# Two probability blocks of each group transposed by way of DRAM, and bucket codes put in place in three transfers a pair: attention and routed experts on one Trainium2 core

## The chip, the cores and the metric

One core of a Trainium2 chip runs the whole program. The metric is device time in microseconds of one launch, the median of several runs. The engines are TensorE (PE, with its weight loads PEld), VectorE (DVE), ScalarE (ACT), GpSimd (POOL) and SyncE (SP), which here only issues transfers.

## The reference

Attention over 4 batches of 8 heads, 768 rows of 64 numbers, restricted to keys in the same hash bucket, then a layer of 8 experts of which each token uses one. Core lines:

```
q_bits = (np.einsum('bhsd,dk->bhsk', q, proj) > 0)      # 6 bits a row; k the same
mask = q_bucket[:, :, :, None] == k_bucket[:, :, None, :]
scores = np.where(mask, scale * q @ k.T, -1e9)
attn = exp(scores - max) / (sum + 1e-9);  out = attn @ v
x = out as rows of 512
e = argmax(x @ w_gate);  y = gate * relu(x @ w1[e]) @ w2[e]
```

## The kernel before

The first 60% of the time is attention. It runs over 16 pairs of heads (4 batches of 4 pairs), each pair in two groups (g=0, 1) of 384 query rows. A group is six steps, one for each block of 128 queries of one head (`blocks`, L508). In pairs 1 to 14 the order of blocks (query block, head) is (1,0), (0,0), (1,1), (0,1), (2,0), (2,1), so the steps n=1 and n=3 hold query block 0 of both heads.

For a block, `scores` (L215) makes 128 x 768 scores on TensorE with four matmuls (L220, L221). L221 adds the low halves of the numbers and, in rows 64 to 75 of its operands q2 and k2, the bucket codes of queries and keys, times a large number, which is the mask. VectorE takes the row maximum (L223) and two small steps (L224, L225), ScalarE the exponential (L235). Scores have two PSUM buffers, so scores of block i+2 wait for the exponential of block i. The products with v (`av`, L272) need the probabilities with keys on partitions. There are two ways to turn them. `transposes` (L255): six 128 x 128 transposes on TensorE (L260), copied out of PSUM by ScalarE in two pieces (L263). `move` (L239): the exponential writes a tile `pd`, SyncE sends it to DRAM in four transfers (L245), fetches it back in another order in one (L248), and VectorE finishes with 32 x 32 transposes (L251, `turn`). Which steps of a group go the second way stands in `MOVES` (L503): step n=1 in pairs 1 to 14, with 28 blocks in all.

The main loop (L742 on) writes out the order on TensorE, VectorE, ScalarE and SyncE by hand. At step i it first calls the `turn` of a block moved five steps earlier, then the transfers that are due: out at the block's own step, back two steps later. Then come scores of block i+2, the exponential of i+1, the transposes of i, and in odd steps the products of one query block of the group before. At n=3 the finished output of an earlier group is transposed (L310) or, for a batch's last pair, its routing logits are made (L332), with small VectorE and ScalarE pieces of the routing in the steps that follow. At n=3 of early groups a transfer fills part of the expert rows with zeros (`prefill`, L116).

The operands of the next pair are prepared meanwhile (`PREPARE`). `pair_codes` at (g=0, n=1) computes codes on TensorE (L143), compares on VectorE (L145) and scales on GpSimd (L146). `q_operands` and `k_operands` split numbers on GpSimd. `code_rows` sends 12 rows of codes into each of q2 and k2 for each half of 384 columns, eight transfers a pair (L171).

Of the kernel before, what the change touches and what calls it, by code (L numbers as in the profile page):

```python
# [8 lines left out]
F32 = mybir.dt.float32  # L9
F32R = mybir.dt.float32r  # L10
# [8 lines left out]
P = 128  # L19
B, H, S, D = 4, 8, 768, 64  # L20
# [5 lines left out]
BITS = 6  # L26
NCODE = 2 * BITS
BIG = float(2.0 ** 60)
# [25 lines left out]
def bf(ap):  # L54
    return ap.bitcast(F32)
# [3 lines left out]
def lsh_attention_moe_kernel(ctx, tc, qkd, q2d, k2d, v, pjbd, wg, w1, w2, ident_in, tri_in, cols_in, eoff_in, ids_in, out):  # L59
    nc = tc.nc  # L60
    V, A, G, PE, SY = nc.vector, nc.scalar, nc.gpsimd, nc.tensor, nc.sync
# [6 lines left out]
    const = ctx.enter_context(tc.tile_pool(name="const", bufs=1))  # L68
    dram = ctx.enter_context(tc.tile_pool(name="dram", bufs=1, space=DRAM))
    xs = dram.tile([E * XROWS, ROW], F32, name="xs")  # L70
    moved = [dram.tile([P, 4, KQ], F32, name=f"moved{x}") for x in range(2)]
    writes = iter(range(6 * B * NPAIR))

    ident = const.tile([P, P], F32, name="ident")
    pj = const.tile([P, 32], F32, name="pj")
    cols = const.tile([P, 3], F32, name="cols")
# [16 lines left out]
    opp = att.enter_context(tc.tile_pool(name="opp", bufs=4))  # L93
# [23 lines left out]

    operands = {}
    codes = {}
    later = []  # L120

    def in_turn(ins):
# [15 lines left out]
    def pair_codes(pr):  # L138
# [6 lines left out]
        V.tensor_scalar(out=cr, in0=cps[:, 0:384], scalar1=0.0, scalar2=cols[:, 0:1], op0=ALU.is_gt, op1=ALU.subtract)  # L145
        in_turn(G.tensor_scalar(out=cr, in0=bf(cr), scalar1=cols[:, 1:2], scalar2=None, op0=ALU.mult))  # L146

    def q_operands(pr, hh):
        qk = operands[pr][0][hh][0]
        q1 = opp.tile([P, S], F32R, name="q1")  # L150
        q2 = opp.tile([P, S], F32R, name="q2")
        in_turn(G.tensor_copy(out=q1[0:D], in_=qk[0:D]))
        in_turn(G.tensor_tensor(out=q1[D:P], in0=qk[0:D], in1=bf(q1[0:D]), op=ALU.subtract))
        in_turn(G.tensor_copy(out=q2[0:D], in_=qk[0:D]))
        operands[pr][0][hh] += [q1, q2]

    def k_operands(pr, hh):
        qk = operands[pr][0][hh][0]
        k1 = opp.tile([P, S], F32R, name="k1")
        k2 = opp.tile([P, S], F32R, name="k2")  # L160
        in_turn(G.tensor_copy(out=k1[D:P], in_=qk[D:P]))
        in_turn(G.tensor_tensor(out=k2[0:D], in0=qk[D:P], in1=bf(k1[D:P]), op=ALU.subtract))
        in_turn(G.tensor_copy(out=k1[0:D], in_=qk[D:P]))
        operands[pr][0][hh] += [k1, k2]

    def code_rows(pr, hh):
        _, q2, _, k2 = operands[pr][0][hh][1:]
        for x in range(2):
            for j, t in enumerate((q2, k2)):
                r0 = 64 * x + 32 * hh + NCODE * j  # L170
                SY.dma_start(out=bf(t[D:KM, 384 * x:384 * x + 384]), in_=bf(codes[pr][r0:r0 + NCODE]))  # L171

    KM = D + NCODE

# [325 lines left out]
        return [logits, gather_heads, total]  # L500

    NPR = B * NPAIR
    MOVES = {}  # L503
    for pr in range(1, NPR - 1):
        for g in range(2):
            MOVES[(pr, g)] = (1,)

    def blocks(pr, g):  # L508
        if (pr, g) in MOVES:
            return [(1, 0), (0, 0), (1, 1), (0, 1), (2, 0), (2, 1)], ((1, 0, 2), (1, 2, 0))[len(MOVES[(pr, g)]) - 1]  # L510
        b = [(jj, hh) for jj in range(3) for hh in range(2)]
        return sorted(b, key=lambda x: x[::-1]) if (pr, g) == (0, 0) else b, (0, 1, 2)

# [18 lines left out]
    V.tensor_copy(out=run, in_=eoff[:, 1])  # L532
    SY.dma_start(out=ids, in_=ids_in)
    for hh in range(2):
        operands[0][0][hh] += [opp.tile([P, S], F32R, name=n) for n in ("q1", "q2", "k1", "k2")]
    PREPARE = (
        {(0, 1): [(pair_codes, ())], (0, 3): [(q_operands, (0,)), (k_operands, (0,))], (0, 5): [(q_operands, (1,)), (k_operands, (1,)), (code_rows, (0,))],
         (1, 1): [(code_rows, (1,))]},
        {(0, 0): [(q_operands, (0,))], (0, 1): [(pair_codes, ())], (0, 2): [(k_operands, (0,))], (0, 4): [(q_operands, (1,))],
         (0, 5): [(code_rows, (0,))], (1, 0): [(k_operands, (1,))], (1, 1): [(code_rows, (1,))]},  # L540
        {(0, 0): [(q_operands, (0,))], (0, 1): [(pair_codes, ())], (0, 2): [(k_operands, (0,))], (0, 3): [(q_operands, (1,))],
         (0, 5): [(k_operands, (1,)), (code_rows, (0,)), (code_rows, (1,))]})
    grp = {}
    soft = {}
    probs = {}
# [196 lines left out]
    for i, (pr, g, jj, hh) in enumerate(steps):  # L742
        n = i % 6
# [62 lines left out]
        if last:  # L806
            if n == 1:
# [4 lines left out]
                c0, c1, c2 = last_route(sums, o)  # L812
            elif n == 2:
                av(pr, g, 0, o)
                r = route(B - 1, 0)
# [203 lines left out]
    bufs = iter(range(1, 2 * E))  # L1019
# [119 lines left out]
    with tc.If(nc.values_load(spare[0:1, E:E + 1], min_val=0, max_val=max(most), skip_runtime_bounds_check_because=why) > 0):  # L1139
# [10 lines left out]
        for e in range(E):  # L1150
            rows_apart("xs", G.indirect_dma_start(out=xs, out_offset=bass.IndirectOffsetOnAxis(ap=row[:, e:e + 1], axis=0),
                                                  in_=pad.rearrange("p g w -> p (g w)"), in_offset=None))
# [7 lines left out]
def layout(q, k, v, proj, moe_w_gate, moe_w1, moe_w2):  # L1160
    import numpy as np
    a = {}
    qd = q.reshape(B * H, S, D).transpose(0, 2, 1)
    kd = k.reshape(B * H, S, D).transpose(0, 2, 1)
    a["qkd"] = np.concatenate([qd, kd], axis=1)
    a["q2d"] = np.concatenate([qd[0:2], qd[0:2]], axis=1)
    a["k2d"] = np.concatenate([kd[0:2], kd[0:2]], axis=1)
    a["v"] = np.ascontiguousarray(v.reshape(B * NPAIR, 2, NB, P, D).transpose(0, 3, 2, 1, 4).reshape(B * NPAIR, P, NB, 2 * D))
    pj = np.zeros((P, 32), proj.dtype)
    for hh in range(2):  # L1170
        for r in range(2):
            pj[hh * D:hh * D + D, hh * NCODE + r * BITS:hh * NCODE + r * BITS + BITS] = proj
    a["pjbd"] = pj
    wg = np.zeros((P, NPAIR, 32), moe_w_gate.dtype)
    for pi in range(NPAIR):
        for hh in range(2):
            wg[hh * D:hh * D + D, pi, hh * E:hh * E + E] = moe_w_gate[(2 * pi + hh) * D:(2 * pi + hh) * D + D]
    a["wg"] = wg

    a["w1"] = np.ascontiguousarray(moe_w1.reshape(E, NG, NDC, SQ, F).transpose(0, 2, 1, 3, 4).reshape(E, DM, F))  # L1180
    a["w2"] = np.ascontiguousarray(moe_w2.reshape(E, F, NG, NDC, SQ).transpose(0, 1, 3, 2, 4).reshape(E, F, DM))
    a["ident"] = np.eye(P, dtype=np.float32)
    a["tri"] = np.triu(np.ones((P, P), np.float32), 1)
    cols = np.zeros((P, 3), np.float32)
    cols[:, 1] = 1.0
    for g in range(4):
        cols[32 * g + BITS:32 * g + NCODE + BITS, 0] = 1.0
        cols[32 * g + NCODE:32 * g + 2 * NCODE, 1] = BIG
    cols[D:D + BITS, 2] = cols[D + 32:D + 32 + BITS, 2] = 1.0
    a["cols"] = cols  # L1190
    eo = np.zeros((P, 4, E), np.float32)
    eo[:, 0] = E - np.arange(E)
    eo[:, 1] = np.arange(E) * XROWS
    eo[:, 2] = CAPS
    eo[:, 3] = E - np.array(RANK)
    a["eoff"] = eo
    tok = np.arange(B * NB)[None, :, None] * P + np.arange(P)[:, None, None]
    first = [np.broadcast_to(np.where(np.arange(P) % SQ < m, 0, NOROW)[:, None, None], (P, 1, NG)) for m in range(4, SQ, 4)]
    a["ids"] = np.concatenate([tok * NG + np.arange(NG)] + first, axis=1).astype(np.int32)
    return a  # L1200
# [14 lines left out]
```

## Time and profile before

| what | value |
|---|---|
| time, median of 3 runs | 757.94 us (754.29 to 761.68) |
| profiled execution, own time | 751.84 us |
| its span | 749.6 us |
| TensorE busy | 725.8 us (97%) |
| VectorE, ScalarE, GpSimd busy | 508.1, 462.2, 409.9 us |

Busy times are means over attention and experts, which have different limits, and matmul records overlap. What a step costs is read from the starts of consecutive rows of one engine, and what it waits for from the bracket at a row's end: the idle time ahead of it and who ended it.

### The profile page before, as it was taken

How to read it: one execution, taken by the hardware profiler on the slowest of the kernel's cores; microseconds unless marked ns; L12 is line 12 of the kernel's file. 1: busy time of each engine (PE TensorE's matmuls, PEld its weight loads, DVE VectorE, ACT ScalarE, POOL GpSimd, SP SyncE). 2: the span in 40 equal slices, each digit the busy share in tenths (PEclk: the TensorE clock that was granted, in tenths of full speed). 3: DMA queues.
4: the chain of work that ended last, by engine and by line, in shares of the span. 5: the costliest groups of instructions: out<-in, count | busy, mean ns of one | idle time of the engine just before them, and what ended most of it. 6: DMA issues, size and time to landing. Idle time of an engine off the chain costs nothing.

```text
span 749.6 us, 16423 instructions
## 1 busy us (share of the span) xinstructions
PE 725.8 (97%) x6039; PEld 644.1 (86%) x6039; DVE 508.1 (68%) x1138; ACT 462.2 (62%) x945; POOL 409.9 (55%) x401
## 2 busy tenths in 40 slices
PE   6999999999999999999999999999999999999996
PEld 3788888887888887888878788999999999999994
DVE  6677776787776787776787777674647465665741
ACT  6787887877877768877767784352424344344430
POOL 2864674395665395565385551105655647455571
PEclk9999999999999999999999999999999999999999
DMA  5436657345333345333434630747465666657621
GB/s 163 122 102 191 195 166 212 112 127 159 114 93 111 114 131 154 115 91 110 132 116 152 175 96 31 167 146 193 129 192 135 179 156 190 195 175 206 183 68 45
DMA packets 70841, 105.70 MB, mean 141 GB/s; under 512 B 9148, under 2 KB 45534, under 8 KB 70752
## 3 DMA queue, kind: packets, MB, share of 16 engines
q1 hardware_dynamic: 65776, 91.88, 43.3%
q0 software_dynamic: 4976, 12.69, 4.7%
q8 instruction: 49, 0.80, 0.5%
q14 instruction: 40, 0.33, 0.1%
HBM read 71.18 MB, written 31.39 MB: 137 GB/s over the span
## 4 chain that ended last, share of the span: by engine, by line
PE 50%; issue 20%; POOL 13%; DVE 7%; DMA 4%; ACT 3%; SPq 1%; POOLq 0%; DVEq 0%; ACTq 0%
PE o L278 16%; PE t L260 11%; POOL y L990 11%; PE s L220 10%; PE s L221 8%; DVE m L223 3%; POOL yo L988 2%; PE misc L310 2%; ACT p L235 2%; PE misc L143 2%; DMA y<-yo,tok 1%; DMA xr<-xs 1%; DMA xre<-xs 1%; DVE m L225 1%; PE misc L332 1%
## 5 line engine op out<-in xcount | busy, mean ns | idle before, releaser
L223 DVE TENSOR_REDUCE m<-s 128x1 f32<-128x768 f32 x192 | 183.4, 955 | 59.5 <-PE s L221 44.2
L235 ACT ACTIVATE p<-s,m 128x768 f32<-128x768 f32 x164 | 163.3, 996 | 50.8 <-DVE m L225 40.6
L263 ACT COPY pt<-t 128x384 f32<-128x384 f32 x328 | 140.5, 482 | 43.1 <-PE t L260 42.8
L220 PE MATMUL s<-k,q 128*128 128x512 f32 (+1 forms) x384 | 149.1, 388 | 10.1 <-ACT p L235 9.1
L278 PE MATMUL o<-pt,vt 128*64 128x128 f32 x2304 | 146.8, 277 | 0.0
L278 PEld LDWEIGHTS o<-pt,vt 128*64 128x64 f32 x2304 | 123.8, 137 | 15.2 <-issue 11.4
L260 PE MATMUL t<-ident,p 128*128 128x128 f32 x984 | 134.8, 273 | 0.0
L221 PE MATMUL s<-k,q 76*128 76x512 f32 (+1 forms) x384 | 124.3, 344 | 0.1
L990 POOL DMA_INDIRECT y<-yo,tags x88 | 103.5, 1176 | 24.9 <-issue 22.6
L260 PEld LDWEIGHTS t<-ident,p 128*128 128x128 f32 x984 | 112.4, 140 | 1.5 <-issue 1.2
L220 PEld LDWEIGHTS s<-k,q 128*128 128x128 f32 x384 | 73.4, 191 | 46.8 <-ACT p L235 17.7
L948 ACT ACTIVATE hh<-hps 128x352 fp32r<-128x352 f32 (+3 forms) x56 | 28.0, 500 | 96.6 <-PE hps L962 96.6
L673 DVE TENSOR_TENSOR wlo<-wraw,whi 128x1024 fp32r<-128x1024 f32 x60 | 73.3, 1223 | 18.5 <-ACT whi L668 18.5
L221 PEld LDWEIGHTS s<-k,q 76*128 76x128 f32 x384 | 74.0, 193 | 9.4 <-ACT k L196 0.6
L981 PE MATMUL hps<-hh,whi 128*128 128x448 f32 (+9 forms) x224 | 75.7, 338 | 0.0
L981 PE MATMUL hps<-hl,whi 128*128 128x436 f32 (+6 forms) x224 | 75.6, 338 | 0.0
L981 PE MATMUL hps<-hh,wlo 128*128 128x436 f32 (+6 forms) x224 | 75.6, 338 | 0.0
L962 PE MATMUL hps<-xh,whi 128*128 128x352 f32 (+3 forms) x224 | 75.2, 336 | 0.0
L962 PE MATMUL hps<-xl,whi 128*128 128x428 f32 (+6 forms) x224 | 74.9, 335 | 0.0
L962 PE MATMUL hps<-xh,wlo 128*128 128x428 f32 (+6 forms) x224 | 74.7, 334 | 0.0
L988 POOL TENSOR_TENSOR yo<-yt,tags 128x512 f32<-128x512 f32 (+3 forms) x25 | 23.2, 951 | 84.1 <-DVE yt L983 84.0
L949 DVE SCALAR_TENSOR_TENSOR hl<-hps,hh 128x352 fp32r<-128x352 f32 (+3 forms) x56 | 31.7, 565 | 45.4 <-ACT hh L948 44.7
(222 smaller groups left out, 1175.1 us busy)
## 6 DMA issues: line engine op xcount, KB each, us to landing
wraw<-w SPq DMA_DIRECT2D x64, 512.0 KB
qk<-qkd SPq DMA_DIRECT2D x30, 384.0 KB
moved<-pd SPq DMA_DIRECT2D x112, 96.0 KB
pq<-moved SPq DMA_DIRECT2D x28, 384.0 KB
xs<-zrow SPq DMA_DIRECT2D x8, 910.0 KB
vt<-v SPq DMA_DIRECT2D x16, 384.0 KB
xr<-xs SPq DMA_DIRECT2D x12, 178.8 KB
xr<-xs SPq DMA_DIRECT2D x8, 227.5 KB
```

The lines of the kernel that those rows point to most:

```text
L220: PE.matmul(out=s[:, c0:c1], lhsT=q1[:, qs], rhs=k1[:, c0:c1], start=True, stop=False)
L221: PE.matmul(out=s[:, c0:c1], lhsT=q2[0:KM, qs], rhs=k2[0:KM, c0:c1], start=False, stop=True)
L223: V.reduce_max(out=m[:, 0:1], in_=s[:, 0:S], axis=AX.X)
L235: A.activation(to, of, AF.Exp, bias=m[:, 2:3], scale=m[:, 1:2], accum_out=sums[:, idx:idx + 1])
L260: PE.transpose(out=t[:, i * P:i * P + P], in_=p[:, kc * P:kc * P + P], identity=ident)
L263: A.copy(out=dst, in_=src)
L278: PE.matmul(out=o[hh * D:hh * D + D, jj * P:jj * P + P], lhsT=vt[:, kc, hh * D:hh * D + D], rhs=pt[:, hh, kc], start=kc == 0, stop=kc == N ...
L673: loeng.tensor_tensor(out=lo[:, i:i + step], in0=cell["t"], in1=bf(hi[:, i:i + step]), op=ALU.subtract)
L962: PE.matmul(out=hps[:, 0:w], lhsT=wt[:, c, fs], rhs=xt[:, c, 0:w], start=n == 0, stop=n == 3 * NDC - 1)
L981: PE.matmul(out=yps[:, 0:w], lhsT=wt[:, f, ds], rhs=ht[:, 0:w], start=n == 0, stop=n == 3 * NFC - 1)
L988: G.tensor_tensor(out=yo[:, 0:i1 - i0], in0=yt[:, i0:i1], in1=tags[:, i0:i1, 1:2].broadcast_to([P, i1 - i0, SEG]), op=ALU.mult)
L990: rows_apart("out", G.indirect_dma_start(out=out_seg, out_offset=bass.IndirectOffsetOnAxis(ap=tags[:, i, 0:1].bitcast(I32), axis=0), in_=y ...
```

## The change

In pairs 1 to 13 step n=3 is moved like step n=1, so that query block 0 goes by way of DRAM for both heads: 54 blocks in place of 28. The order of products in such a group becomes blocks 1, 2, 0, in steps 1, 3 and 5 of the next group. The second `turn` stands at step 2 of the next group. The codes no longer go from SBUF to SBUF in eight transfers: the tile of codes goes to DRAM in one (`codes_out`) and comes back in two (`codes_back`), each for 12 partitions and all four second operands, q2 and k2 of both heads, which are now one tile `c2`. The host layout places the codes of queries and keys 16 rows apart for that.

```diff
+    coded = [dram.tile([P, 384], F32, name=f"coded{x}") for x in range(2)]
...
+    def seconds(pr):
+        if pr not in second:
+            second[pr] = opp.tile([P, 4, S], F32R, name="c2", bufs=2)
+        return second[pr]
...
-        q2 = opp.tile([P, S], F32R, name="q2")
+        q2 = seconds(pr)[:, 2 * hh]
...
-        k2 = opp.tile([P, S], F32R, name="k2")
+        k2 = seconds(pr)[:, 2 * hh + 1]
...
-    def code_rows(pr, hh):
-        _, q2, _, k2 = operands[pr][0][hh][1:]
+    def codes_out(pr):
+        SY.dma_start(out=coded[pr % 2], in_=bf(codes[pr]))
+
+    def codes_back(pr):
+        way = coded[pr % 2].rearrange("(x y c) w -> c y x w", x=2, c=16)
         for x in range(2):
-            for j, t in enumerate((q2, k2)):
-                r0 = 64 * x + 32 * hh + NCODE * j
-                SY.dma_start(out=bf(t[D:KM, 384 * x:384 * x + 384]), in_=bf(codes[pr][r0:r0 + NCODE]))
+            SY.dma_start(out=bf(seconds(pr)[D:KM, :, 384 * x:384 * x + 384]), in_=way[0:NCODE, :, x])
...
+    MOVED = {(14, 0): (1,), (14, 1): (1,)}
     MOVES = {}
     for pr in range(1, NPR - 1):
         for g in range(2):
-            MOVES[(pr, g)] = (1,)
+            MOVES[(pr, g)] = MOVED[(pr, g)] if (pr, g) in MOVED else (1, 3)
...
-            return [(1, 0), (0, 0), (1, 1), (0, 1), (2, 0), (2, 1)], ((1, 0, 2), (1, 2, 0))[len(MOVES[(pr, g)]) - 1]
+            return [(1, 0), (0, 0), (1, 1), (0, 1), (2, 0), (2, 1)], ((1, 0, 2), (1, 2, 0), (1, 0, 2))[len(MOVES[(pr, g)]) - 1]
...
-        {(0, 0): [(q_operands, (0,))], (0, 1): [(pair_codes, ())], (0, 2): [(k_operands, (0,))], (0, 4): [(q_operands, (1,))],
-         (0, 5): [(code_rows, (0,))], (1, 0): [(k_operands, (1,))], (1, 1): [(code_rows, (1,))]},
+        {(0, 0): [(q_operands, (0,))], (0, 1): [(pair_codes, ())], (0, 2): [(k_operands, (0,))], (0, 4): [(q_operands, (1,)), (codes_out, ())],
+         (1, 0): [(k_operands, (1,)), (codes_back, ())]},
```

Lines of the changed kernel are eight or so higher than those of before: L260 is L268 there, L278 is L286, L251 is L259, L223 is L231, L145 is L147.

TensorE, step n=3 of group g=0 of pair 6, before: scores of a block two steps ahead, the six transposes, the products of one query block (24 matmuls, 12 for each head, printed as x12), three small transposes.

```order
L220 MATMUL s<-k_2461,q_2373 128x512
L221 MATMUL s<-k_2462,q_2374 128x512
L220 MATMUL s<-k_2461,q_2373 128x256
L221 MATMUL s<-k_2462,q_2374 128x256
L260 MATMUL t<-ident,p 128x128 x6
L278 MATMUL o<-pt,vt 64x128 x12
L310 MATMUL misc<-ident,ot 128x128 x3
```

The same step of the changed kernel:

```order
L228 MATMUL s<-k_2387,q_2301 128x512
L229 MATMUL s<-c_2165 128x512
L228 MATMUL s<-k_2387,q_2301 128x256
L229 MATMUL s<-c_2165 128x256
L286 MATMUL o<-pt,vt 64x128 x12
L318 MATMUL misc<-ident,ot 128x128 x3
```

The six transposes are gone and the products follow the scores.

VectorE, group g=0 of pair 6, around the compare of codes (cr); m<-s is a row maximum. Before:

```order
L223 TENSOR_REDUCE m<-s 128x1
L224 TENSOR_SCALAR m<-m 128x1
L225 TENSOR_SCALAR m<-m 128x1
L145 TENSOR_SCALAR cr<-misc,cols 128x384
L223 TENSOR_REDUCE m<-s 128x1
```

The changed kernel there:

```order
L231 TENSOR_REDUCE m<-s 128x1
L232 TENSOR_SCALAR m<-m 128x1
L233 TENSOR_SCALAR m<-m 128x1
L147 TENSOR_SCALAR cr<-misc,cols 128x384
L259 STREAM_TRANSPOSE pt<-pq 128x768
L231 TENSOR_REDUCE m<-s 128x1
```

The transpose of the second moved block stands between the compare and the maximum of the next scores.

SyncE, from the codes of one pair through its group g=1 and into the next pair, in the middle of the stage; moved<-pd is a block going out, pq<-moved coming back, qk<-qkd a load of a head. Before:

```order
L171 DMA q_2231<-cr 12x384
L171 DMA k_2301<-cr 12x384
L135 DMA vt<-v 128x768
L245 DMA moved_62<-pd 32x4x192 x4
L171 DMA q_2374<-cr 12x384
L171 DMA k_2462<-cr 12x384
L171 DMA q_2374<-cr 12x384
L171 DMA k_2462<-cr 12x384
L248 DMA pq<-moved_62 128x768
L130 DMA qk<-qkd 128x768 x2
L245 DMA moved_61<-pd 32x4x192 x4
L248 DMA pq<-moved_61 128x768
```

The changed kernel:

```order
L174 DMA coded_61<-cr 128x384
L256 DMA pq<-moved_64 128x768
L137 DMA vt<-v 128x768
L179 DMA c_2165<-coded_61 12x4x384 x2
L253 DMA moved_63<-pd 32x4x192 x4
L256 DMA pq<-moved_63 128x768
L253 DMA moved_64<-pd 32x4x192 x4
L132 DMA qk<-qkd 128x768 x2
L256 DMA pq<-moved_64 128x768
L253 DMA moved_63<-pd 32x4x192 x4
L256 DMA pq<-moved_63 128x768
```

The transfers of codes stand around the load of v, and the loads of heads now stand ahead of the second block's transfer back.

## Rows read from the trace of the kernel before

**Rows 1.** Windows: stretch, length, busy us by engine, granted clock, DMA share, GB/s.

```profile
180.00:220.00 40.00, 40.00 (x406) 34.22 (x405) 29.54 (x66) 32.12 (x70) 24.82 (x25) 1.00 0.34 97
...
380.00:400.00 20.00, 18.55 (x193) 16.10 (x193) 17.06 (x48) 15.25 (x35) 16.36 (x17) 1.00 0.47 145
```

**Rows 2.** Timeline of TensorE, pair 7, g=0: start, length, line, tiles, count.

```profile
206.55 0.48 PE L220 MATMUL s<-k,q 128*128 128x512 f32 x1
...
207.42 1.53 PE L278 MATMUL o<-pt,vt 128*64 128x128 f32 x24
...
209.67 0.50 PE L220 MATMUL s<-k,q 128*128 128x512 f32 x1
...
211.06 0.48 PE L220 MATMUL s<-k,q 128*128 128x512 f32 x1
...
212.59 1.53 PE L278 MATMUL o<-pt,vt 128*64 128x128 f32 x24
...
214.36 0.48 PE L220 MATMUL s<-k,q 128*128 128x512 f32 x1
```

**Rows 3.** Page, costliest groups: busy us, mean ns of one, idle before.

```profile
L260 PE MATMUL t<-ident,p 128*128 128x128 f32 x984 | 134.8, 273 | 0.0
```

**Rows 4.** Timeline of VectorE and ScalarE, the same group.

```profile
209.81 0.62 DVE L145 TENSOR_SCALAR cr<-misc,cols 128x384 fp32r<-128x384 f32 x1 [0.81 <-PE misc L143]
...
210.75 0.96 DVE L223 TENSOR_REDUCE m<-s 128x1 f32<-128x768 f32 x1 [0.32 <-PE s L221]
...
212.24 0.99 ACT L235 ACTIVATE p<-s,m 128x768 f32<-128x768 f32 x1 [0.37 <-DVE m L225]
...
218.09 0.97 DVE L251 STREAM_TRANSPOSE pt<-pq 128x768 f32<-128x768 f32 x1
```

**Rows 5.** Timeline, pair 12: scores that waited for an exponential.

```profile
361.96 0.99 ACT L235 ACTIVATE p<-s,m 128x768 f32<-128x768 f32 x1 [0.87 <-DVE oh L355]
...
363.10 0.50 PE L220 MATMUL s<-k,q 128*128 128x512 f32 x1 [0.28 <-ACT p L235]
```

**Rows 6.** Timeline, pair 7, g=1: a maximum and later scores.

```profile
223.54 0.96 DVE L223 TENSOR_REDUCE m<-s 128x1 f32<-128x768 f32 x1 [0.97 <-PE s L221]
...
227.17 0.48 PE L220 MATMUL s<-k,q 128*128 128x512 f32 x1
```

**Rows 7.** Timeline of TensorE, pair 12, g=0: products to scores with routing logits between.

```profile
350.13 1.53 PE L278 MATMUL o<-pt,vt 128*64 128x128 f32 x24
...
352.38 0.50 PE L220 MATMUL s<-k,q 128*128 128x512 f32 x1
```

**Rows 8.** Timeline, pair 13, g=0: the second maximum after the codes, and later scores.

```profile
380.19 0.95 DVE L223 TENSOR_REDUCE m<-s 128x1 f32<-128x768 f32 x1
...
383.30 0.48 PE L220 MATMUL s<-k,q 128*128 128x512 f32 x1
```

**Rows 9.** Timeline of SyncE's issues, pair 7, and GpSimd's wait for a head.

```profile
206.20 2.06 SPq L245 DMA_DIRECT2D moved<-pd  x4
...
209.91 0.34 SPq L248 DMA_DIRECT2D pq<-moved  x1
...
211.87 0.78 SPq L171 DMA_DIRECT2D q<-cr  x1
...
218.83 0.36 SPq L135 DMA_DIRECT2D vt<-v  x1
...
225.25 0.90 SPq L130 DMA_DIRECT2D qk<-qkd  x2
...
229.00 0.82 POOL L152 CAST q<-qk 64x768 fp32r<-64x768 f32 x1 [5.72 <-DMA qk<-qkd]
```

**Rows 10.** Page, DMA issues: count and KB each.

```profile
xs<-zrow SPq DMA_DIRECT2D x8, 910.0 KB
```

**Rows 11.** By tile and by line: ns minimum, median, maximum, first and last start.

```profile
L251 DVE STREAM_TRANSPOSE pt<-pq x28: 934/968/972, 54.0 to 431.3; 128x768 f32<-128x768 f32 x28
...
L374 DVE TENSOR_TENSOR pos<-pos,ohb x7: 172/175/1533, 147.1 to 463.4; 128x24 f32<-128x24 f32 x7
```

More of the change, by code (lines that the diff above doesn't have):

```diff
@@ L119, in lsh_attention_moe_kernel @@
     codes = {}
+    second = {}
     later = []
@@ L534, in lsh_attention_moe_kernel @@
     for hh in range(2):
-        operands[0][0][hh] += [opp.tile([P, S], F32R, name=n) for n in ("q1", "q2", "k1", "k2")]
+        q1, k1 = (opp.tile([P, S], F32R, name=n) for n in ("q1", "k1"))
+        operands[0][0][hh] += [q1, seconds(0)[:, 2 * hh], k1, seconds(0)[:, 2 * hh + 1]]
     PREPARE = (
-        {(0, 1): [(pair_codes, ())], (0, 3): [(q_operands, (0,)), (k_operands, (0,))], (0, 5): [(q_operands, (1,)), (k_operands, (1,)), (code_rows, (0,))],
-         (1, 1): [(code_rows, (1,))]},
-        {(0, 0): [(q_operands, (0,))], (0, 1): [(pair_codes, ())], (0, 2): [(k_operands, (0,))], (0, 4): [(q_operands, (1,))],
-         (0, 5): [(code_rows, (0,))], (1, 0): [(k_operands, (1,))], (1, 1): [(code_rows, (1,))]},
+        {(0, 1): [(pair_codes, ())], (0, 3): [(q_operands, (0,)), (k_operands, (0,))], (0, 5): [(q_operands, (1,)), (k_operands, (1,)), (codes_out, ())],
+         (1, 1): [(codes_back, ())]},
+        {(0, 0): [(q_operands, (0,))], (0, 1): [(pair_codes, ())], (0, 2): [(k_operands, (0,))], (0, 4): [(q_operands, (1,)), (codes_out, ())],
+         (1, 0): [(k_operands, (1,)), (codes_back, ())]},
         {(0, 0): [(q_operands, (0,))], (0, 1): [(pair_codes, ())], (0, 2): [(k_operands, (0,))], (0, 3): [(q_operands, (1,))],
-         (0, 5): [(k_operands, (1,)), (code_rows, (0,)), (code_rows, (1,))]})
+         (0, 4): [(codes_out, ())], (0, 5): [(k_operands, (1,)), (codes_back, ())]})
     grp = {}
@@ L1171, in layout @@
         for r in range(2):
-            pj[hh * D:hh * D + D, hh * NCODE + r * BITS:hh * NCODE + r * BITS + BITS] = proj
+            pj[hh * D:hh * D + D, 16 * hh + r * BITS:16 * hh + r * BITS + BITS] = proj
     a["pjbd"] = pj
@@ L1186, in layout @@
     for g in range(4):
-        cols[32 * g + BITS:32 * g + NCODE + BITS, 0] = 1.0
-        cols[32 * g + NCODE:32 * g + 2 * NCODE, 1] = BIG
+        cols[32 * g + BITS:32 * g + NCODE, 0] = cols[32 * g + 16:32 * g + 16 + BITS, 0] = 1.0
+        cols[32 * g + 16:32 * g + 16 + NCODE, 1] = BIG
     cols[D:D + BITS, 2] = cols[D + 32:D + 32 + BITS, 2] = 1.0
```

## Prediction

> **What bounds the kernel now.** I read the windows first. In the attention stage TensorE is busy for all of a plain stretch, and where it is not (18.55 of 20.00 us) the granted clock still stands at 1.00, the 2.4 GHz level, so idle time of that size costs no clock here [rows 1]. Busy matmul time hides waits, since matmuls overlap, so I then read the starts in the timeline. From one score to the next, TensorE's rows of group g=0 of pair 7 follow each other with nothing between them that waits for another engine: the step without products ends 1.39 us after it began (209.67 to 211.06), and step 3, with scores, transposes, products and three small transposes, takes 3.30 us (211.06 to 214.36) [rows 2]. So TensorE's order of work sets the length of a plain group, and what leaves TensorE there leaves the time, unless another engine's chain is nearly as long. There are 32 groups. The change touches 26, both groups of pairs 1 to 13.
>
> **What is removed.** Each of the 26 groups loses the six transposes of step 3 on TensorE and two copies on ScalarE. Their price is read from starts. With transposes, the products of step 3 begin 1.53 us after the scores did (211.06 to 212.59). In step 1, where the block is already moved, they begin 0.87 us after (206.55 to 207.42) [rows 2]. The difference, 0.66 us, is what a group can gain, 26 x 0.66 = 17.2 us in all. The page's group of this line gives 273 ns as the mean of one [rows 3], and six times that would be 1.64 us. The Trainium skill (TensorE: Matmul & The Clock Gate, Part 4: PE-mode transpose) gives about 275 ns for one transpose in a kernel's context, with the array's access latency as most of it. By that figure the sum would be 26 x 1.65 = 43 us, by the row's starts it is 17.2 us; the starts decide, since a latency that overlaps is not paid six times. The two copies are taken at nothing: ScalarE is not what TensorE waits for in these rows.
>
> **What is added on VectorE.** One transpose a group, 0.97 us [rows 4], in VectorE's program order at the start of step 2 of the next group, ahead of the maximum (L223) of that step's scores. What is queued behind it: that maximum, the exponential, and the scores of step 4, which need the PSUM buffer that the exponential frees. The chain from a maximum's start to those scores is 1.49 us to the exponential's start (210.75 to 212.24) [rows 4], 0.99 us of it, and 0.15 us from its end to the scores that waited for it (362.95 to 363.10) [rows 5], 2.63 us together.
>
> In g=1 the transpose falls into a gap: before the maximum at 223.54 VectorE was idle for 0.97 us, waiting for scores [rows 6]. The maximum stays, so the scores could start at 223.54 + 2.63 = 226.17. TensorE, 0.66 us earlier than its 227.17, comes at 226.51. Nothing is lost, a gain of 0.66 us.
>
> In g=0 the compare that makes the codes (L145, 209.81 for 0.62 us) stands ahead of it. The transpose then runs from 210.43 to 211.40, and the maximum moves from 210.75 to 211.40. The scores of step 4 can start at 211.40 + 2.63 = 214.03, and TensorE would come at 214.36 - 0.66 = 213.70 [rows 2, 4]. So 0.33 us is given back and 0.33 us stays. The upper bound is no delay, 0.66 us. Successive VectorE rows overlap a little, so I take 0.41 us, near the lower bound.
>
> Six of the 13 pairs also carry routing. In the first of each two (pairs 4, 8, 12) the logits stand in step 3 of g=0: from products to scores it is 2.25 us (350.13 to 352.38) [rows 7] instead of 1.77 us (212.59 to 214.36) [rows 2]. The extra 0.48 us covers the 0.33 us above, so both groups gain 0.66 us. In the second (pairs 5, 9, 13) more VectorE work follows: the second maximum at 380.19 would move by the same 0.65 us, to 380.84, and its scores to 383.47, where they started at 383.30 [rows 8]. There g=0 loses 0.17 us, and g=1, whose waits I cannot add up from rows, gains between 0 and 0.66 us. I take 0.5 us for such a pair, bounds -0.2 and 1.3.
>
> Sum: 7 x (0.66 + 0.41) + 3 x 1.32 + 3 x 0.5 = 7.5 + 4.0 + 1.5 = **13.0 us**.
>
> **What is added on the queues.** A second block a group goes to DRAM in four transfers and comes back in one. On SyncE that is 2.06 + 0.34 us, 4.8 us a pair. The eight code transfers, up to 0.78 us each, 6.2 us, are replaced by one of 128 partitions (0.34 us, as the transfer back of a block) and two of 12 partitions (0.78 us, as now), 1.9 us [rows 9]. So SyncE has 4.8 + 1.9 - 6.2 = 0.5 us more to issue in a pair, and that is taken at nothing, since what it issues is wanted later, as follows. The slot of a moved block, from the first transfer out to its transpose, is 218.09 - 206.20 = 11.89 us [rows 4, 9], and 11.2 us once steps are shorter. The way there is 3.71 us from the first transfer out to the transfer back (206.20 to 209.91), and at most 3.75 us for that to land, taken from the two heads, twice its size, which were asked for at 225.25 and let GpSimd start at 229.00 [rows 9]. That is 7.5 us, in time. In g=1 the two heads (384 KB each) now stand ahead of the second block's transfer back: another 3.75 us, 11.2 us, just in time by a bound that counts each latency twice. In three g=1 groups (pairs 1, 2 and 3) a zero fill of 910 KB [rows 10] stands there as well: 910 / 768 x 3.75 = 4.4 us more, at most 13 us in all if nothing overlaps, nothing if it does. I take nothing.
>
> Codes: the transfer back stands behind the load of v, issued at 218.83 when the last products of the pair before are done. With 0.36 us for that and 1.56 us for the two issues it is out by 220.8 and, by the heads' 3.75 us, landed by 224.5; the next pair's first scores need it at 226.5 [rows 6, 9]. Two us of cover. That the four second operands of a pair now share one buffer of two changes nothing in how many pairs deep they are held, and is taken at nothing. If the cover were gone TensorE would wait once a pair, 13 times. The transfers out of the g=1 block start some 0.9 us later, inside its slot.
>
> **The rivals.** (A) As summed, a gain of 13.0 us, own range 10.5 to 17.2 us: 745 us, 740.7 to 747.4.
>
> (B) The cover is thinner: the three zero-fill groups cost about 2 us each, or the routing pairs give all back. Gain 4 to 10 us, some 751 us. For it: the bounds just given. Against it: the product steps now follow the steps before without a gap [rows 2].
>
> (C) The change takes six transposes away and the time stays, because scores, maximum, exponential and the second transpose become the loop. Per two steps the loop is 1.08 us from scores to maximum (209.67 to 210.75) and 2.63 us, 3.71 us; with the 0.97 us transpose in series 4.68 us, against 1.39 + 3.30 = 4.69 us now [rows 2, 4]. Gain 26 x 0.01 us, 758 us. For it: in g=0 half of that is so. Against it: the gap of 0.97 us in g=1 is not in the loop.
>
> (D) Slower: the second block lands late. The transpose waits in order on VectorE, and the maxima, the exponentials and TensorE with them. It decides once the way exceeds 11.2 us by 13.0 / 26 = 0.5 us in all groups. At 12.0 us it costs 26 x 0.8 = 20.8 us, less 13.0 us: 766 us. For it: 11.2 us in g=1 by the bound. Against it: 7.5 us in g=0, and no VectorE transpose waits for a transfer today.
>
> (E) GpSimd holds the transposes up. One small VectorE operation, L374, took 1533 ns once and 172 ns at best, while the 28 transposes took 934 to 972 ns, GpSimd busy beside many of them [rows 11]. If each new one were held for 1.36 us, 26 x 1.36 = 35 us less 13.0 us: 780 us. The Trainium skill (SBUF — State Buffer, SBUF: two separate sides) says that VectorE and GpSimd share one port pair under an exclusive lock, taken by VectorE's two-port forms and for two SBUF inputs; a transpose with one input that runs at 0.97 us each time shows no such wait, so the trace speaks against it here.
>
> **How the numbers follow.** The profiled execution took 751.84 us, 749.6 us of span and 2.2 us around it, below all three timed runs (754.29 to 761.68). A gain of 13.0 us gives 738.8 us beside it and, on the median of 757.94 us, 744.9 us, which I give as 745 us. Chances: A 0.58, B 0.19, C 0.13, D 0.08, E 0.02. One per cent, 7.6 us, is about what a measurement of this kernel can tell from no change. A is faster by more than that, half of B too; the other half and C lie within; D and E are slower. That is 0.68 faster, 0.22 within, 0.10 slower. The range runs from A's upper gain less the 3.7 us by which runs lie beside their median (740.7 - 3.7 = 737 us) to B's smallest gain (754 us). It leaves out D, E and most of C, 0.2.
>
> **What would show it.** TensorE's distance from scores to products in step 3 should be 0.87 us in all 26 groups, and from the scores of step 3 to those of step 4 a plain group should take 2.64 us where it took 3.30 us, in g=1, and about 2.9 us in g=0. VectorE's transposes should number 54 at 0.97 us, none with an idle time that a transfer ended; one such wait in most groups would show D. The scores of step 4 in g=0 should show a wait for the exponential of 0.2 to 0.3 us. If g=0 and g=1 both keep their length, C holds. If g=0 loses nothing, VectorE's order there was priced too high. Wrong altogether would be a longer step 3, or a wait on codes at the first scores of a pair.

## The result, and the profile after

| what | before | after |
|---|---|---|
| median of 20 runs | 757.48 us (751.30 to 765.17) | 749.54 us (745.51 to 753.41) |
| ratio, 95% interval | | 0.9911 (0.9883 to 0.9939) |
| profiled execution, own time | 751.84 us | 748.05 us |
| its span | 749.6 us | 745.9 us |

The changed kernel is faster by 0.9%, 6.7 us by the ratio (4.6 to 8.9 us by its interval). The forecast was 745 us, a gain of 13.0 us. The 20 runs of before lie in two bunches, 11 from 751 to 758 us and 9 from 761 to 765 us (in its runs beside the experiments every one above 761 us shows a granted clock of 0.985 or less, all others 0.989 or more); against the median of the first bunch, 754.6 us, the gain is 5.1 us. The two profiled executions lie only 3.8 us apart, since the one of before is near the lower end of its runs. What follows is read from these two profiles.

The page of after: its span, then busy time of each engine.

```profile
span 745.9 us, 16241 instructions
...
PE 714.8 (96%) x5883; PEld 630.2 (84%) x5883; DVE 527.6 (71%) x1164; ACT 444.0 (60%) x893; POOL 409.8 (55%) x401
...
PEclk9999989999999999999999999999999999999998
```

TensorE has 156 matmuls fewer (6039 to 5883), 26 times six transposes, and VectorE is busy for 19.5 us more (508.1 to 527.6). The row of the granted clock has a new 8 in its sixth slice, which will matter.

TensorE's rows of pair 7, g=0, which answer [rows 2].

```profile
212.93 0.50 PE L228 MATMUL s<-k,q 128*128 128x512 f32 x1
...
214.31 0.48 PE L228 MATMUL s<-k,q 128*128 128x512 f32 x1
...
215.19 1.53 PE L286 MATMUL o<-pt,vt 128*64 128x128 f32 x24
...
217.07 0.51 PE L228 MATMUL s<-k,q 128*128 128x512 f32 x1
```

Step 3 goes from 214.31 to 217.07, 2.76 us where it was 3.30 us, and the products stand 0.88 us behind the scores where it was 1.53 us. VectorE and ScalarE in the same step, which answer [rows 4]:

```profile
213.06 0.62 DVE L147 TENSOR_SCALAR cr<-misc,cols 128x384 fp32r<-128x384 f32 x1 [0.81 <-PE misc L145]
213.60 0.97 DVE L259 STREAM_TRANSPOSE pt<-pq 128x768 f32<-128x768 f32 x1
214.49 0.92 DVE L231 TENSOR_REDUCE m<-s 128x1 f32<-128x768 f32 x1
...
215.94 0.99 ACT L243 ACTIVATE p<-s,m 128x768 f32<-128x768 f32 x1 [0.81 <-DVE m L233]
```

The transpose stands between compare and maximum. The exponential ends at 216.93, and the scores of 217.07 start 0.14 us later, which fits a wait for it; the run with the transpose later, below, shows that VectorE's order sets this start.

For a table by group I took the start of the first matmul of each block's scores from TensorE's timeline and added the six distances of a group. All but three of the 26 groups became shorter or kept their length within 0.1 us (where a cell holds one number for several groups it is their middle one; second pairs have g=0 and g=1 apart):

| group | before, us | after, us | gain of all such groups, us |
|---|---|---|---|
| plain, g=1 (7) | 12.82 | 12.16 | 4.6 |
| plain, g=0 (5: pairs 1, 6, 7, 10, 11) | 13.56 | 13.07 (12.93 in pair 1) | 2.5 |
| first pair with routing (5: pair 4 g=1, pairs 8, 12) | 14.73, 14.15 | 14.07, 13.46 | 3.4 |
| second pair with routing (6: pairs 5, 9, 13) | 14.73, 14.80 | 14.78, 14.15 | 1.8 |
| pair 2, g=0 | 13.56 | 15.68 | -2.1 |
| pair 3, g=0 | 13.56 | 19.11 | -5.6 |
| pair 4, g=0 | 14.73 | 15.86 | -1.1 |

The 23 groups gain 12.3 us. The other three lose 8.8 us where 0.5, 0.5 and 0.66 us were to be gained: 10.4 us are missing there. With them the sum would have been 14.0 us.

They are the groups behind the three zero fills that stand in g=1. The waits view of after: who waited for whom, us in total, times, longest.

```profile
PEld misc L145 <- DMA qk<-qkd: 7.3, 3, 3.2
...
PE misc L145 <- DMA qk<-qkd: 5.2, 3, 2.5
```

TensorE waits three times, at the matmul of the codes (L145), for the load of the second head. That is a transfer which the prediction had not asked about. SyncE's issues ahead of the longest (block out, first head, fill, second head, block back):

```profile
89.90 1.85 SPq L253 DMA_DIRECT2D moved<-pd  x4
91.79 0.45 SPq L132 DMA_DIRECT2D qk<-qkd  x1
92.28 0.43 SPq L117 DMA_DIRECT2D xs<-zrow  x1
92.75 3.33 SPq L132 DMA_DIRECT2D qk<-qkd  x1
96.32 0.85 SPq L256 DMA_DIRECT2D pq<-moved  x1
```

And TensorE, with its weight load's own wait:

```profile
97.33 0.83 PE L145 MATMUL misc<-qk,pj 128*32 128x384 f32 x2
100.63 1.50 PE L145 MATMUL misc<-qk,pj 128*32 128x384 f32 x6 [2.46 <-DMA qk<-qkd]
102.06 0.80 PE L228 MATMUL s<-k,q 128*128 128x512 f32 x1
...
103.51 1.48 PE L268 MATMUL t<-ident,p 128*128 128x128 f32 x6
104.64 0.78 PE L228 MATMUL s<-k,q 128*128 128x512 f32 x1
...
108.33 0.48 PE L228 MATMUL s<-k,q 128*128 128x512 f32 x1
...
109.13 0.82 PE L268 MATMUL t<-ident,p 128*128 128x128 f32 x6
```

The codes behind the first of the three waits, for comparison:

```profile
72.13 0.84 PE L145 MATMUL misc<-qk,pj 128*32 128x384 f32 x6 [1.82 <-DMA qk<-qkd]
```

The weight load ahead of the slow codes:

```profile
100.63 0.19 PEld L145 LDWEIGHTS misc<-qk,pj 128*32 128x32 f32 x6 [3.16 <-DMA qk<-qkd]
```

The second head is asked for at 92.75, its issue alone takes 3.33 us, and TensorE starts on it at 100.63, 7.9 us later. Behind the wait everything on TensorE is slow: six transposes take 1.48 us where they take 0.82 us at 109.13. The windows say why (columns as in [rows 1]):

```profile
96.00:101.00 5.00, 2.54 (x29) 1.49 (x31) 1.37 (x4) 2.16 (x4) 3.43 (x3) 0.92 1.05 344
101.00:104.00 3.00, 3.00 (x13) 1.75 (x8) 1.68 (x3) 0.00 (x0) 1.02 (x1) 0.50 0.25 64
104.00:108.00 4.00, 4.00 (x33) 3.44 (x31) 2.56 (x7) 2.05 (x5) 3.79 (x5) 0.63 0.90 264
108.00:112.00 4.00, 4.00 (x39) 3.63 (x39) 3.02 (x7) 2.92 (x7) 3.71 (x5) 1.00 0.97 291
```

The transfers fill all DMA engines (share 1.05, 344 GB/s) while TensorE waits. From 101 to 104 us the granted clock is 0.50, the 1.2 GHz level, and by 108 us it is back at 2.4 GHz. What that cost is read from the rows: codes 1.50 instead of 0.84 us, step 2 2.58 (102.06 to 104.64) instead of 1.39 us, step 3 3.69 (104.64 to 108.33) instead of 2.76 us, together 2.8 us. So of the 10.4 us, 2.8 us are a slow clock, and the 7.6 us that remain are put down to the waits (7.3 us in the waits view).

### The profile page after: what moved, and what is told of

Same layout as the page of the kernel before. It is cut to its first block, busy times and chain, and to the rows that moved or that the text cites. A ratio compares the mean times of both kernels' runs of the same rounds, so it can differ in the third digit from the quotient of the medians.

```text
span 745.9 us, 16241 instructions
## 1 busy us (share of the span) xinstructions
PE 714.8 (96%) x5883; PEld 630.2 (84%) x5883; DVE 527.6 (71%) x1164; ACT 444.0 (60%) x893; POOL 409.8 (55%) x401
## 5 line engine op out<-in xcount | busy, mean ns | idle before, releaser
L231 DVE TENSOR_REDUCE m<-s 128x1 f32<-128x768 f32 x192 | 182.4, 950 | 42.0 <-PE s L229 25.6
L243 ACT ACTIVATE p<-s,m 128x768 f32<-128x768 f32 x138 | 137.0, 993 | 52.4 <-DVE m L233 38.4
L286 PE MATMUL o<-pt,vt 128*64 128x128 f32 x2304 | 147.6, 278 | 0.0
L271 ACT COPY pt<-t 128x384 f32<-128x384 f32 x276 | 118.4, 482 | 45.1 <-PE t L268 43.9
L286 PEld LDWEIGHTS o<-pt,vt 128*64 128x64 f32 x2304 | 124.6, 137 | 14.7 <-issue 7.4
L229 PE MATMUL s<-c 76*128 76x512 f32 (+1 forms) x384 | 124.3, 344 | 0.0
L268 PE MATMUL t<-ident,p 128*128 128x128 f32 x828 | 114.8, 275 | 0.1
L268 PEld LDWEIGHTS t<-ident,p 128*128 128x128 f32 x828 | 95.4, 141 | 1.8 <-issue 1.2
L229 PEld LDWEIGHTS s<-c 76*128 76x128 f32 x384 | 73.9, 193 | 9.3 <-ACT c L204 0.4
L159 POOL CAST q<-qk 64x768 fp32r<-64x768 f32 x30 | 24.7, 822 | 76.3 <-DMA qk<-qkd 37.5
```

Source lines behind the costliest of these rows:

```text
L229: PE.matmul(out=s[:, c0:c1], lhsT=q2[0:KM, qs], rhs=k2[0:KM, c0:c1], start=False, stop=True)
L231: V.reduce_max(out=m[:, 0:1], in_=s[:, 0:S], axis=AX.X)
L243: A.activation(to, of, AF.Exp, bias=m[:, 2:3], scale=m[:, 1:2], accum_out=sums[:, idx:idx + 1])
L268: PE.transpose(out=t[:, i * P:i * P + P], in_=p[:, kc * P:kc * P + P], identity=ident)
L271: A.copy(out=dst, in_=src)
L286: PE.matmul(out=o[hh * D:hh * D + D, jj * P:jj * P + P], lhsT=vt[:, kc, hh * D:hh * D + D], rhs=pt[:, hh, kc], start=kc == 0, stop=kc == N ...
```

## The experiments

Theory 1: the step gains are as forecast, and what is missing is lost behind the zero fills of g=1 (pairs 1, 2, 3), since the second head's load stands behind a second block (384 KB out) and the fill (910 KB). Rivals: the codes by way of DRAM carry part of the gain or the loss; VectorE's new transpose costs more than 0.1 us; the loss comes with the amount of data and would stay in another order.

**The loss without the change.** The kernel before, with a second zero fill of 910 KB into a spare tensor ahead of the second head, in those three groups and nowhere else.

```diff
+    extra_rows = dram.tile([C, ROW], F32, name="extra_rows")
...
+            if i in (21, 33, 45):
+                extra_fill()
```

> The kernel before, with three more zero fills of 910 KB, to a tensor that nobody reads, issued right behind the fill in g=1 of pairs 1, 2 and 3, ahead of the second head. No second block is moved. Theory 1 (the order of bytes ahead of the second head decides): L143 waits for the second head in g=0 of pairs 2, 3 and 4, 0.5 to 3 us each, although the change is absent. If the second block matters by itself (SyncE's issues, VectorE's order), no such waits, and these groups keep 13.56, 13.56 and 14.73 us.

One run: 772.25 us, span 770.0 us. Its waits view:

```profile
PEld misc L148 <- DMA qk<-qkd: 10.6, 3, 4.5
PE misc L148 <- DMA qk<-qkd: 8.5, 3, 3.8
```

The three groups behind take 15.48, 19.69 and 21.56 us, where before took 13.56, 13.56 and 14.73 us, and two of the three waits are longer than the 3 us that were expected at most. So a transfer put ahead of the second head makes this wait at this place, without a second moved block in the kernel. The mean granted clock of this run is 0.985, that of the profile of before 0.998.

**Heads first.** The changed kernel with the two heads asked for at steps 1 and 2 of g=1 instead of 3 and 4, ahead of the fill.

```diff
-        if g == 1 and n in (3, 4) and pr + 2 < NPR:
-            if n == 3:
+        if g == 1 and n in (1, 2) and pr + 2 < NPR:
+            if n == 1:
...
-            operands[pr + 2][0].append(load_head(pr + 2, n - 3))
+            operands[pr + 2][0].append(load_head(pr + 2, n - 1))
```

> The changed kernel, with the loads of the next two heads issued at steps 1 and 2 of g=1 in place of 3 and 4, so ahead of the second block's transfers and of the zero fill. Theory 1 (in the three groups with a zero fill in g=1 the second head lands behind the second block and the fill, and TensorE waits for it at the codes of the next group; that costs 10.6 us in the profile of the changed kernel, slower clock behind the waits included): the three waits of L145 for a head vanish, groups g=0 of pairs 2, 3 and 4 take 13.0, 13.0 and 14.1 us between first scores instead of 15.7, 19.1 and 15.9, the clock stays at 1.00 around 100 us, ratio to before 0.978 (0.973 to 0.983). Theory 2 (what is late there is a product of the change itself, the codes or the moved block, not the head): the waits stay or turn into waits of VectorE's transpose for pq or of scores for codes, ratio 0.988 to 0.994.

743.01 us, ratio 0.9809 (0.9753 to 0.9864). No row waits for a head at L145, and g=0 of pairs 2 and 4 take 13.07 and 14.08 us. But pair 3 takes 14.48 and 16.52 us, and the waits view has a new row:

```profile
DVE pt L259 <- DMA pq<-moved: 5.2, 4, 3.2
```

The longest of its four waits in VectorE's timeline:

```profile
112.91 0.98 DVE L259 STREAM_TRANSPOSE pt<-pq 128x768 f32<-128x768 f32 x1 [3.21 <-DMA pq<-moved]
```

The clock falls behind this one too, to 0.60 from 117 to 121 us. Part of the loss is gone and part has moved to the next transfer in the line, the second block's way back. The transfer that the prediction had feared is late only in this order.

**Fill last.** The changed kernel with the fill of g=1 at step 5, behind both heads and the transfer back.

```diff
-        if 9 <= i <= 51 and n == 3:
+        if 9 <= i <= 53 and n == (5 if g else 3):
```

> The changed kernel with the zero fill of a group g=1 issued at step 5, behind both heads and the second block's transfer back, in place of step 3. If the order at the transfers is what costs (the second head behind the fill), the waits for heads at the codes matmul go: pairs 2 to 4, g=0, at 13.1, 13.1 and 14.1 us in place of 15.7, 19.1 and 15.9, ratio 0.978 to 0.981. If the amount of data is what costs, wherever it stands, other transfers wait in its place (the first block of the next group, the load of v) and the ratio stays near 0.988 to 0.991.

744.39 us, ratio 0.9883 (0.9827 to 0.9939). The waits for heads are gone (g=0 of pairs 2 to 4: 13.06, 13.30 and 14.08 us). In their place VectorE waits for blocks:

```profile
DVE pt L259 <- DMA pq<-moved: 5.5, 4, 3.0
```

Group g=1 of pair 2 takes 13.51 and of pair 3 16.25 us, where after has 12.16 us. The fill of g=1 now stands only four steps ahead of the fill of the next g=0. So theory 1 had the place, and the rival the reason: with the fill and two blocks there is more to carry there than lands in time, and in both other orders another tile was late.

**One block there.** The changed kernel with one moved block, as before, in g=1 of pairs 1, 2 and 3, and two in the other 23 groups.

```diff
-    MOVED = {(14, 0): (1,), (14, 1): (1,)}
+    MOVED = {(14, 0): (1,), (14, 1): (1,), (1, 1): (1,), (2, 1): (1,), (3, 1): (1,)}
```

> The changed kernel, but only one block moved in g=1 of pairs 1, 2 and 3, the groups whose zero fill stands by the heads. Codes still go by way of DRAM. Theory 1: without the second block's 768 KB in and out the heads land in time as before; the waits vanish, three gains of 0.66 us are given up, so about 2 us less than with the heads first: ratio 0.980 (0.975 to 0.985). Theory 2, codes: the codes' new way is unchanged here, so the waits stay: ratio 0.990 to 0.995.

740.92 us, ratio 0.9781 (0.9723 to 0.9839). The same kernel once more, beside later runs:

> The kernel with one moved block in g=1 of pairs 1 to 3 once more, beside the two runs above on the same chip: 0.976 to 0.982 of before again, and the base that the later rows are set against.

739.73 us, ratio 0.9803 (0.9758 to 0.9849). Its waits for the head and for the block's return:

```profile
DVE pt L259 <- DMA pq<-moved: 1.6, 1, 1.6
...
PEld misc L145 <- DMA qk<-qkd: 0.5, 1, 0.5
```

```profile
60.00:75.00 15.00, 15.00 (x161) 12.74 (x161) 11.31 (x26) 11.78 (x27) 5.88 (x6) 1.00 0.67 198
88.00:108.00 20.00, 20.00 (x196) 17.07 (x192) 15.07 (x32) 15.92 (x35) 12.62 (x12) 1.00 0.84 247
```

In the first two stretches where after waited, TensorE is busy for all of the time at clock 1.00. Some waiting is left by the third fill: pair 3, g=1 takes 13.59 and 13.69 us in the two profiles and pair 4, g=0 15.26 and 14.72 us. Giving up three gains of 0.66 us brings back most of the 10.4 us: the 26 groups are 10.0 and 10.6 us shorter than before, and this version beats both kernels.

**Both mends.** Heads first and one block there.

```diff
-    MOVED = {(14, 0): (1,), (14, 1): (1,)}
+    MOVED = {(14, 0): (1,), (14, 1): (1,), (1, 1): (1,), (2, 1): (1,), (3, 1): (1,)}
...
-        if g == 1 and n in (3, 4) and pr + 2 < NPR:
+        if g == 1 and n in (1, 2) and pr + 2 < NPR:
```

> The changed kernel with both mends of the zero-fill groups: head loads at steps 1 and 2, and one moved block in place of two in g=1 of pairs 1 to 3. If the three groups behind the fills are all that the change lost (10.6 us with the clock), pairs 2 to 4, g=0, take 12.9, 13.1 and 14.1 us, nothing waits for a head or for a block's transfer back, and the gain is 15 to 18 us: ratio 0.976 to 0.980. If something else holds it, it stays at the 0.981 that moving the heads alone gave.

741.22 us, ratio 0.9820 (0.9776 to 0.9864). Pairs 2 to 4, g=0, take 12.92, 12.92 and 14.08 us, as expected; against the expectation one moved block is still late by 1.5 us, and pair 3, g=1 takes 13.58 us for 12.82. The 26 groups together are 11.7 us shorter than before. The whole is no faster than with one block alone. In this profile the end of attention took longer (pair 14 g=1 15.68, pair 15 g=0 17.92 us, before 14.70 and 15.70 us), with the clock at the lower level behind it. That place is taken up below.

**The codes.** Once without them (two blocks a group, codes in eight transfers as before), and once alone (one block a group, codes by way of DRAM).

```diff
-            MOVES[(pr, g)] = (1,)
+            MOVES[(pr, g)] = (1, 3) if pr < NPR - 2 else (1,)
```

> Two blocks moved in pairs 1 to 13, but codes put in place as before, eight transfers of 12 partitions a pair from SBUF to SBUF. Theory 1: the three waits for heads stay, and SyncE has about 4 us more to issue in a pair, in front of transfers that have slack: the same ratio as the changed kernel within 0.4%, 0.988 to 0.995. Rival (the codes' new way is what makes room for the second block on SyncE): the blocks come back later, VectorE's second transposes wait for pq in most groups at 0.5 us or more, ratio 1.00 or higher.

751.40 us, ratio 0.9919 (0.9876 to 0.9962), with the same three waits (15.42, 19.38 and 15.95 us). Moved blocks are late as well, though in two groups and not in most: VectorE's transposes wait for them four times, 3.0 us in all, and g=0 of pairs 11 and 12 take 13.94 and 15.11 us, where after has 13.10 and 14.08 us.

```diff
-            MOVES[(pr, g)] = MOVED[(pr, g)] if (pr, g) in MOVED else (1, 3)
+            MOVES[(pr, g)] = MOVED[(pr, g)] if (pr, g) in MOVED else (1,)
```

> The changed kernel with one moved block in every group, as before: of the change only the codes by way of DRAM are left. Theory 1 (the time comes from the six transposes, codes cost and bring nothing): ratio 1.000, 0.996 to 1.004, plain steps as before (step 3 at 3.31 us in both halves). Theory 2 (a part of the 6.7 us comes from the five transfers a pair that SyncE no longer issues): 0.996 or less. In the groups of the zero fills the second head is asked for behind one block and the fill, as before: theory 1 expects no wait for it there.

751.79 us, ratio 0.9978 (0.9951 to 1.0004). Step 3 is 3.30 and 3.32 us as before, and the 26 groups together differ from before by 0.1 us. So the codes' way alone changes no step, and the blocks' gain and their loss behind the fills are there without it. Beside two blocks a group it keeps two groups from being late, 1.9 us in this profile.

**The transpose later.** The second block's VectorE transpose at step 4 of the next group instead of 2.

```diff
-            turns.append((i + 5, turn))
+            turns.append((i + (7 if n == 3 else 5), turn))
```

> The changed kernel with the second block's VectorE transpose at step 4 of the next group in place of step 2. If the transpose behind the compare of codes is what leaves step 3 of g=0 at 2.76 us in place of 2.66, that goes: 0.1 us in 7 plain groups, and in the groups with routing 0.2 to 0.6 us each, 1 to 3 us in all, ratio to before 0.987 to 0.990. If VectorE's order there costs nothing beyond the 0.1 us, the ratio stays at 0.991. The waits for heads, 10.6 us in pairs 2 to 4, stay in both.

751.53 us, ratio 0.9950 (0.9910 to 0.9991): no gain. TensorE's starts of scores in pair 7, from step 2 of g=0 on:

```profile
212.01 0.50 PE L228 MATMUL s<-k,q 128*128 128x512 f32 x1
213.40 0.48 PE L228 MATMUL s<-k,q 128*128 128x512 f32 x1
216.04 0.48 PE L228 MATMUL s<-k,q 128*128 128x512 f32 x1
217.41 0.48 PE L228 MATMUL s<-k,q 128*128 128x512 f32 x1
220.42 0.50 PE L228 MATMUL s<-k,q 128*128 128x512 f32 x1
222.03 0.50 PE L228 MATMUL s<-k,q 128*128 128x512 f32 x1
```

Step 3 is 2.64 us (213.40 to 216.04) instead of 2.76 us, so the 0.1 us in g=0 is VectorE's order, as supposed. But step 0 of the next group becomes 1.61 us (220.42 to 222.03) instead of 1.39 us, in both halves: twice 0.22 us lost for 0.1 us gained. Most of the forecast 1 to 3 us was wrong: it left out what stands behind the transpose at its new place.

This run also bears on the clock. It waits for the heads as after does, and for longer:

```profile
128.91 0.15 PEld L145 LDWEIGHTS misc<-qk,pj 128*32 128x32 f32 x6 [3.50 <-DMA qk<-qkd]
```

```profile
125.00:135.00 10.00, 7.19 (x66) 4.49 (x61) 4.54 (x11) 3.68 (x8) 7.13 (x7) 1.00 0.73 221
```

The clock stays at 1.00 behind a wait of 3.50 us, where it fell behind one of 3.16 us in after.

**The end of attention.** In after, VectorE waits there for the rows of the first expert, which it transposes in its program order ahead of maxima (in before it waits 2.4 us for them):

```profile
421.77 0.48 DVE L644 STREAM_TRANSPOSE xt<-xre 128x288 f32<-128x288 f32 x1 [2.92 <-DMA xre<-xs]
```

These transposes were moved two steps later, once in the kernel with one block there and once in the changed kernel.

```diff
-{(0, 3): [wf[0], xf[0]], (0, 5): [wf[1], xf[1]], (1, 1): [xf[2], wf[2]],
+{(0, 3): [wf[0]], (0, 5): [xf[0], wf[1]], (1, 0): [xf[1]], (1, 1): [xf[2], wf[2]],
```

> One moved block in place of two in g=1 of pairs 1 to 3, and VectorE's transposes of the first expert's rows (xt from xre) two steps later, where the rows have landed. Theory 1 (the wait for these rows at the end of attention, 2.0 to 3.7 us in the profiles, is lost time that the change brings forward but doesn't cause): pair 14, g=1, step 5 and pair 15, g=0, step 1 take about 3.0 and 3.1 us in place of 4.2 to 5.9 and 3.1 to 4.8; 1 to 5 us less than with one block alone, ratio to before 0.972 to 0.978. Theory 2 (the end of attention is held by the weights of the first expert behind the rows): the wait moves to a later step and the time stays, 0.978 to 0.982.

739.68 us, ratio 0.9793 (0.9746 to 0.9840), beside 739.73 us without the edit.

> The changed kernel with VectorE's transposes of the first expert's rows two steps later, nothing else. If the end of attention is a loss beside the waits for heads, pair 14, g=1, step 5 and pair 15, g=0, step 1 fall from 5.1 and 4.6 us to about 3.0 and 3.1, 3 to 4 us, and the ratio to before goes from 0.991 to about 0.987; the 10.6 us in pairs 2 to 4 stay. If the wait only moves on to the weights, 0.991.

747.12 us, ratio 0.9889 (0.9848 to 0.9931), which its interval does not tell from after. In both profiles step 5 of pair 14, g=1 falls to 3.0 us. Step 1 of pair 15, g=0 takes 4.44 us where the kernel with one block had 3.07 us, and 4.69 us where after had 4.60 us. The kernel with one block and this edit:

```profile
419.75 0.98 DVE L259 STREAM_TRANSPOSE pt<-pq 128x768 f32<-128x768 f32 x1 [1.86 <-DMA pq<-moved]
```

The wait has gone on, not to the weights as theory 2 had it, but to the next block on its way back, which stands behind the same loads. There too it is a transfer that is waited for, and moving the first instruction that waits brings nothing that was measured.

## Why the prediction was right, and where it was wrong

The time lay in the forecast range, but not where the sum put it: 13.0 us were forecast and 6.7 us measured. The gains of the groups came out nearly as summed, 12.3 us in 23 groups. The time missed the own range of A (740.7 to 747.4 us). It lay in the whole range because that reached to the smallest gain of rival B, whose loss the sum had taken at nothing.

**What a group gains: right.** 0.66 us was read from starts, not from the 273 ns of [rows 3], and g=1 of all seven plain pairs went from 12.82 to 12.16 us. With the 275 ns that the prediction quoted from a page of the Trainium skill (TensorE: Matmul & The Clock Gate, Part 4: PE-mode transpose) a group would have become 1.65 us shorter; none of the 26 groups gains more than 0.75 us.

**VectorE in g=0: right in mechanism, a little dear.** The order compare, transpose, maximum and the wait of the scores for the exponential are in the rows. The maximum moved from 0.31 us ahead of step 3's scores (210.75, 211.06) to 0.18 us behind them (214.49, 214.31), 0.49 us and not 0.65 us, since rows overlap: the transpose starts 0.54 us after the compare that took 0.62 us, and the maximum 0.89 us after a transpose of 0.97 us. From maximum to scores it is 2.58 us (214.49 to 217.07), forecast 2.63 us. So 0.49 us stayed, where 0.41 us had been taken. The late transpose confirms it: 0.1 us comes back at this place. The wait of 0.2 to 0.3 us that the prediction asked for stands in no bracket; by the starts it is this 0.1 us.

**Pairs with routing: right.** 0.66 and 0.7 us a group in the first ones. In the second ones g=0 lost 0.05 us (forecast 0.17) and g=1 gained 0.48 to 0.75 us, 1.8 us in all where 1.5 us had been taken.

**The queues: the step that failed.** The prediction bounded the zero fill in three g=1 groups by 4.4 us each, "at most 13 us in all if nothing overlaps, nothing if it does", and took nothing. It cost 10.4 us, close to the other bound. Two things were wrong in that step. It looked at the second block's way back only, and not at the second head, which stands behind the same fill and which TensorE itself needs three steps later; the way back was in time in after, as all 54 transposes show:

```profile
L259 DVE STREAM_TRANSPOSE pt<-pq x54: 935/968/978, 53.0 to 426.5; 128x768 f32<-128x768 f32 x54
...
  DMA pq<-moved: 0.3, 1
```

And it chose "overlaps" with no row for it. The trace of before had rows that speak against it. Behind the fills of pairs 1 and 2, g=1, its DMA engines were already full:

```profile
64.00:68.00 4.00, 4.00 (x43) 3.52 (x42) 3.52 (x7) 3.19 (x7) 2.09 (x2) 1.00 1.01 344
88.00:94.00 6.00, 6.00 (x72) 5.31 (x69) 4.54 (x12) 4.97 (x13) 1.88 (x2) 1.00 0.99 295
```

In after the transfers filled them again (share 1.05 at 344 GB/s), so what was queued there could not overlap for free. The Trainium skill (DMA: Bandwidth & Descriptors, Specifications) puts the limit of memory for one core at about 358 GB/s; the 344 GB/s lie just below it, and no run here shows what sets them. From the rows alone: block out, head, fill and head, 384 + 384 + 910 + 384 KB, asked for between 89.90 and 92.75, are 2.11 MB, 6.1 us at 344 GB/s, so the last lands at 96.0 at best, with nothing else in flight. What was outstanding from before and the block back at 96.32 would share the rest, to 100.6; how much each took was not measured.

The second head was also asked for later. In before that was 0.9 us ahead of the scores of step 4 (88.54 and 89.48):

```profile
88.54 0.56 SPq L130 DMA_DIRECT2D qk<-qkd  x1
```

In after it was 3.5 us behind them (92.75 and 89.23), since the first block's transfer back comes later (89.47, in before 87.18) and the second block's four issues stand ahead of the heads. This takes cover away, but alone it makes nothing wait: with the fill last the heads were asked for 2.2 us behind step 4 (90.81 and 88.59) and TensorE waited for none, while in the kernel before with more fill the second head was asked for 0.4 us ahead of step 4 (91.89 and 92.30) and TensorE waited 4.5 us. A sum of bytes in flight against the rate of the fullest window, for each tile that stands behind the new transfer, would have found it.

**The clock: wrong at one place.** The prediction read from [rows 1] that idle time of 1.45 us in 20 costs no clock. That held in the window it read; behind one wait of 3.16 us in after the clock cost 2.8 us.

**SyncE and codes: right that they cost nothing.** The forecast 0.5 us more of issues did not come: the two transfers back take about 0.76 us together (222.05 to 222.81 in pair 7), not 1.56 us, so SyncE issues about as long as before. The first scores of each pair wait for no code row, and with the codes alone no step moves. What the prediction did not count is that the shorter issues help: with the codes as before, two groups more were late.

**The rivals.** B, three zero-fill groups and a gain of 4 to 10 us, is what happened in place and size, though with another tile late and one group at 6.0 us instead of 2 us. A is what the other 23 groups did, and what the version with one block there gives: 15 us below the median of before beside it, of which the 26 groups make up 10.0 to 10.6 us in its profiles; the rest is not traced to a step. C did not happen: g=1 kept its whole gain. D needed blocks late in all groups; in after none is late by more than 0.3 us. E did not: 54 transposes between 935 and 978 ns.

Left open: why the runs of before scatter more than those of after, and when the clock falls behind such a wait and when it does not.

## What to carry to other kernels

When a change adds a transfer to a queue, list every tile that is asked for behind it up to its user, not only the new one, and set the bytes in flight there against the rate that the fullest window shows. A bound of "nothing if it overlaps" needs a row that shows room: read the DMA share of the trace that you have in that stretch, not over the whole stage. Where a few groups have no room, leave the change out there: three groups of 26 lost most of what the others gained, and with those three left as they were the gain came back.

## What the runs showed of the hardware

A wait of TensorE for 3.16 us in after came with some 6.8 us at the 1.2 GHz level (by the windows' mean clocks 0.8 us before 101, 3.0 us to 104, 3.0 us to 108), which cost 2.8 us on top. At the same matmul the clock also fell around waits of 3.33 us (the changed kernel with the first expert's rows later), 3.43 us (codes as before) and 4.45 and 4.33 us (the kernel before with more fill), and it did not fall at one of 3.50 us (the transpose later). SyncE's issue of a load, 0.45 us elsewhere, took 3.33 us while the DMA engines were full, and 3.05 to 3.31 us in the kernel before with more fill.
